# One static order for all five engines, the spatial bias on VectorE and the gate on GpSimd

## The chip, the cores and the metric

The kernel runs on one core of a Trainium2 chip. The metric is the device time of one execution in microseconds (us). Most executions of one kernel agree closely; a run over 1.5% above the fastest of its kernel is called slow, and ratios use fast runs alone. A profiled execution has a span (first to last instruction) of some 1.8 us less than its time (some 2.2 us in the two versions with the bias put back). The profiled run of the kernel before happened to be a slow one (182.71 us, span 180.9), some 5 us above its usual time.

## The reference, cut to what matters

Two parts follow each other. Attention with a decay goes over blocks of tokens with a running state; its output x feeds a gated MLP with a spatial mixing over the tokens of each of four batches.

```python
# attention, per batch and head, block by block
intra = (q @ k.T) * D @ v                  # D: lam**(i-j) where i >= j
inter = (q * lam**(i+1)) @ kv_state
kv_state = lam**block * kv_state + (k * lam**(block-1-i)).T @ v
# MLP, per batch
h = relu(x @ w_in); u, v = halves(h)
v_n = (v - mean(v)) / sqrt(var(v) + 1e-6)
v_s = w_spatial @ v_n + b_spatial
out = (u * v_s) @ w_out
```

The kernel does the attention in 12 steps of 256 tokens, three to a batch.

## The kernel before

Each step is loaded (k, q, v: 1.57 MB, of which k and v come in rows of 256 bytes), cast by GpSimd (kd is k times its decay, qc, vc), transposed by TensorE and copied by ScalarE (kT) and VectorE (qT). The program fixes the order of TensorE, GpSimd and SyncE by hand; the order of ScalarE and VectorE is left to the framework. The steps of the MLP are pv and pu (x times the two halves of w_in), vn (the normalised v), pvs (spatial mixing), po (output). An ask is the instruction by which an engine starts a transfer; the transfer lands later.

The parts that the change and the argument touch:

```python
def load_step(n):                         # SyncE asks: k in two halves, q, then v
    ...
    if n >= 2:
        load_v(n, nc.sync)
...
load_step(0)
load_v(0, nc.scalar, (0,))                # ScalarE asks for half of v 0 at once
load_step(1)
...
load_v(1, nc.sync, (1,))
for n in range(2, 4):
    load_step(n)
...
for g in range(NG):                       # decays of the queries
    last = nc.scalar.activation(out=lq[:, g, :], in_=qpos, func=AF.Exp, scale=logl[:, g:g + 1])
with tc.issue_after(last.ins):
    load_v(0, nc.scalar, (1,))            # the other halves, behind lq
    load_v(1, nc.scalar, (0,))
...
def pvs(b, f):
    ...
        for s in range(NBLK):
            nc.tensor.matmul(out=ps[:, i, 0:HW_], lhsT=vn..., rhs=wt_sb..., ...)
        nc.tensor.matmul(out=ps[:, i, 0:HW_], lhsT=oo128, rhs=bsp_bc[:, cols], ...)   # the bias
    nc.vector.tensor_tensor(out=gT..., in0=ps..., in1=uT..., op=ALU.mult)             # the gate
...
run("""
    mask ck:0 cq:0 ck:1 cv:0 win:1 cq:1 cv:1 c:2 win:0 wsp wout c:3 lk:4 lk:5 lk:6
    T:0 K:0 A:0 T:1 O:0 K:1 A:1 pv:0:0 O:1 T:2 K:2 ...
""")
```

## Time and profile before

| | before |
|---|---|
| time, median (range) | 177.0 us (176.21 to 178.74), 3 runs |
| TensorE busy (PE) | 145.4 us, 80% of the span of 180.9 |
| VectorE (DVE) | 106.0 us, 59% |
| ScalarE (ACT) | 77.3 us, 43% |
| GpSimd (POOL) | 53.2 us, 29% |
| transfers | 28.36 MB, done with all but stores at about 104 us |

The table is to be read with time in mind: none of these shares is near 100%, because the loads hold everything up in the first 44 us and TensorE is full later. The prediction shows the rows that say so.

### The profile page before, as it was taken

To read this page: it belongs to the slowest core of one execution; us is meant where nothing else is said; L and a number is where in the kernel's file an instruction comes from. 1 tells how busy PE (TensorE), PEld (TensorE's weight loads), DVE (VectorE), ACT (ScalarE), POOL (GpSimd) and SP (SyncE) were. 2 spreads that over 40 slices of the span, in tenths; PEclk is the share of its full clock that TensorE was granted. 3 is DMA by queue.
4 is the path that set the end of the run, shared out by engine and by line. 5 is a ranking of instruction groups with operands and counts; after the bars stand their busy time and mean duration, and the time that the engine had idled before them with its cause. 6 is when DMAs were issued, how large, how long until landed. Compare 5 with 4: busy or idle time off the path is not lost.

```text
span 180.9 us, 3629 instructions
## 1 busy us (share of the span) xinstructions
PE 145.4 (80%) x1528; PEld 95.2 (53%) x1540; DVE 106.0 (59%) x182; ACT 77.3 (43%) x88; POOL 53.2 (29%) x50
## 2 busy tenths in 40 slices
PE   0041699399869999997955999999999999999890
PEld 0031566176636665676742655567866645776430
DVE  0712988921652889579998447179994713834400
ACT  2940057237911045677450014756822257660051
POOL 2439639400555566207556702000000000000000
PEclk9999999969987999999997899999999999999997
DMA  3999999999999999999899900630000026000036
GB/s 79 266 224 239 212 243 224 194 202 200 239 226 218 253 216 270 321 263 196 220 238 224 236 5 0 235 116 4 0 4 0 0 104 248 0 0 5 0 126 222
DMA packets 68497, 28.36 MB, mean 157 GB/s; under 512 B 50560, under 2 KB 65536, under 8 KB 68480
## 3 DMA queue, kind: packets, MB, share of 16 engines
q1 hardware_dynamic: 62560, 24.25, 58.2%
q0 software_dynamic: 2512, 2.95, 9.4%
q10 hardware_dynamic: 3408, 0.92, 2.7%
q8 instruction: 12, 0.20, 0.5%
q14 instruction: 5, 0.04, 0.1%
HBM read 24.78 MB, written 6.29 MB: 172 GB/s over the span
## 4 chain that ended last, share of the span: by engine, by line
PE 53%; DVE 17%; DMA 12%; SPq 9%; ACT 3%; issue 1%; POOL 1%; ACTq 0%; POOLq 0%
PE pvs L344 17%; PE po L359 10%; DMA wsp_raw<-in_moe_w_spatial_dram 8%; PE pv L313 8%; PE pu L334 7%; SPq L78 5%; DVE a L228 5%; DMA v_in<-in_v_dram 5%; DVE vn L325 4%; PE pvs L346 3%; PE pt L199 3%; DVE gT L348 2%; SPq L80 2%; DVE st L319 2%; SPq L69 2%; DVE sd L254 2%
## 5 line engine op out<-in xcount | busy, mean ns | idle before, releaser
L344 PE MATMUL pvs<-wt_sb,vn 128*128 128x384 bf16 x192 | 39.8, 343 | 5.2 <-DVE vn L325 5.1
L228 DVE TENSOR_TENSOR a<-pam,amask 128x1024 bf16<-128x1024 f32 x24 | 28.5, 1211 | 3.4 <-PE pam L225 3.4
L183 POOL TENSOR_TENSOR kd<-k_in,ldec 128x1024 bf16<-128x1024 f32 x12 | 23.0, 1917 | 23.2 <-DMA k_in<-in_k_dram 16.2
L344 PEld LDWEIGHTS <-vn 128*128 128x128 bf16 x192 | 19.4, 103 | 19.6 <-DVE vn L325 6.3
L204 ACT ACTIVATE kT<-pt 128x1024 bf16<-128x1024 bf16 x12 | 12.2, 1021 | 38.9 <-PE pt L199 38.9
L348 DVE TENSOR_TENSOR gT<-pvs,uT 128x768 bf16<-128x768 f32 x16 | 15.3, 957 | 19.6 <-PE pvs L346 19.6
L334 PE MATMUL pu<-xT,win_sb 128*128 128x256 bf16 x192 | 24.0, 284 | 2.9 <-DMA win_sb<-in_moe_w_in_dram 2.9
L313 PE MATMUL pv<-win_sb,xT 128*128 128x512 bf16 x89 | 22.0, 380 | 1.9 <-ACT xT L288 1.6
L359 PE MATMUL po<-wout_sb,gT 128*128 128x512 bf16 x91 | 21.7, 379 | 1.4 <-DVE a L228 0.7
L319 DVE BATCH_NORM_STATS2 st<-vh 128x6 f32<-128x512 bf16 x24 | 15.4, 682 | 12.5 <-ACT vh L316 12.3
L334 PEld LDWEIGHTS <-win_sb 128*128 128x128 bf16 x192 | 19.2, 102 | 6.6 <-DMA win_sb<-in_moe_w_in_dram 3.0
L288 ACT ACTIVATE xT<-pat 128x1024 bf16<-128x1024 f32 x12 | 15.8, 1320 | 15.6 <-PE pat L285 15.4
L191 POOL CAST vc<-v_in 128x1024 bf16<-128x1024 f32 x12 | 12.8, 1066 | 28.1 <-DMA v_in<-in_v_dram 20.9
L372 ACT ACTIVATE o<-po 128x1024 f32<-128x1024 f32 x11 | 11.3, 1025 | 18.3 <-PE po L359 18.3
L336 ACT ACTIVATE uT<-pu 128x1024 bf16<-128x1024 f32 x12 | 12.2, 1021 | 10.1 <-PE pu L334 10.1
L316 ACT ACTIVATE vh<-pv 128x1024 bf16<-128x1024 f32 x12 | 12.2, 1021 | 8.2 <-PE pv L313 8.1
L199 PE MATMUL pt<-ident,kd 128*128 128x128 bf16 x96 | 8.2, 234 | 9.1 <-POOL kd L183 9.1
L359 PEld LDWEIGHTS <-gT 128*128 128x128 bf16 x96 | 9.1, 98 | 11.7 <-DVE gT L348 1.3
L313 PEld LDWEIGHTS <-xT 128*128 128x128 bf16 x96 | 8.9, 98 | 11.3 <-ACT xT L288 2.0
L188 POOL CAST qc<-q_in 128x1024 bf16<-128x1024 f32 x12 | 12.9, 1076 | 5.9 <-DMA q_in<-in_q_dram 5.7
L206 DVE TENSOR_TENSOR qT<-pt,lq 128x1024 bf16<-128x1024 bf16 x12 | 8.2, 684 | 10.7 <-ACT kT L204 10.7
L325 DVE TENSOR_SCALAR vn<-vh,mv,rstd 128x512 bf16<-128x512 bf16 x24 | 14.1, 629 | 0.3
(54 smaller groups left out, 142.0 us busy)
## 6 DMA issues: line engine op xcount, KB each, us to landing
k_in<-in_k_dram SPq DMA_DIRECT2D x24, 256.0 KB, 5.3
q_in<-in_q_dram SPq DMA_DIRECT2D x12, 512.0 KB, 6.7
out_dram<-o SPq DMA_DIRECT2D x11, 512.0 KB, 3.1
v_in<-in_v_dram SPq DMA_DIRECT2D x21, 256.0 KB, 6.5
wsp_raw<-in_moe_w_spatial_dram POOLq DMA_DIRECT2D x1, 1152.0 KB, 14.2
win_sb<-in_moe_w_in_dram POOLq DMA_DIRECT2D x2, 512.0 KB, 8.2
v_in<-in_v_dram ACTq DMA_DIRECT2D x3, 256.0 KB, 6.3
wout_sb<-in_moe_w_out_dram POOLq DMA_DIRECT2D x1, 512.0 KB, 17.4
```

What stands on the lines that cost most here:

```text
L183: nc.gpsimd.tensor_tensor(out=kd.rearrange("p c h d -> p h c d"), in0=s["k_in"], in1=ldec.unsqueeze(2).unsqueeze(3).broadcast_to((P, H, 2, ...
L188: nc.gpsimd.tensor_copy(out=qc.rearrange("p m h d -> p h m d"), in_=s["q_in"])
L199: nc.tensor.transpose(out=pt[:, j, g, c * P:(c + 1) * P], in_=src[:, c, 2 * g:2 * g + 2, :].rearrange("p h d -> p (h d)"), identity=ident)
L228: nc.vector.tensor_tensor(out=a_sb[:, i].rearrange("p h g c x -> p (h g) c x"), in0=pam.rearrange("p h g c x -> p (h g) c x"), in1=amask[: ...
L288: nc.scalar.activation(out=xT[b][:, r].rearrange("p g (c d m) -> p (g c) m d", c=2, m=2), in_=po.rearrange("p g c (m d) -> p (g c) m d", m ...
L313: nc.tensor.matmul(out=ps[:, j], lhsT=x[:, r, c, j * P:(j + 1) * P], rhs=win_sb[:, c, DH:DFF], start=(c == 0), stop=(c == NCH - 1))
L319: nc.vector.bn_stats(out=m["st6"][:, t, :], in_=vh[:, t, :])
L325: nc.vector.tensor_scalar(out=m["vn"][:, t, :], in0=vh[:, t, :], scalar1=mv[:, t, 0:1], scalar2=rstd[:, t:t + 1], op0=ALU.subtract, op1=AL ...
L334: nc.tensor.matmul(out=ps[:, f], lhsT=win_sb[:, c, f * P:(f + 1) * P], rhs=x[:, r, c, :], start=(c == 0), stop=(c == NCH - 1))
L344: nc.tensor.matmul(out=ps[:, i, 0:HW_], lhsT=m["vn"][:, s, f * P:(f + 1) * P], rhs=wt_sb[:, s, cols], start=(s == 0), stop=False)
L348: nc.vector.tensor_tensor(out=m["gT"][:, f, :].rearrange("p (i x) -> p i x", i=2), in0=ps[:, :, 0:HW_], in1=m["uT"][:, f, :].rearrange("p ...
L359: nc.tensor.matmul(out=ps[:, j], lhsT=gT[:, c, t * P:(t + 1) * P], rhs=wout_sb[:, c, :], start=(c == 0), stop=(c == NCH - 1))
```

## The change

The intent is to give each engine one static order, made by a list schedule, in which work of three batches interleaves; to take the bias matmuls from TensorE and the gate from VectorE; and to drop the rescaling of the state by using decays counted from the start of the batch. The diff, cut to its core:

```diff
-    ctx.enter_context(tc.manual_schedule(engines={PE, Pool, SP}))
+    ctx.enter_context(tc.manual_schedule(engines={PE, Pool, Activation, DVE, SP}))
 ...
+    def load_v(n):
+        load_kv("v", v, n, nc.scalar if n < 2 else nc.sync)
 ...
+    def key_decays(r): ...        # 6 exponentials instead of 1 (ldec), lm128 and l128 gone
+    def query_decays(r): ...      # 12 instead of 4 (lq)
 ...
-                nc.vector.tensor_tensor(out=sd, in0=prev, in1=lb, op=ALU.mult)
-                nc.vector.tensor_tensor(out=s_sb[:, c], in0=sd, in1=pkv[:, c], op=ALU.add)
+            nc.vector.tensor_tensor(out=s["s"][:, c], in0=prev, in1=s["pkv"][:, c], op=ALU.add)
 ...
-            nc.tensor.matmul(out=ps[:, i, 0:HW_], lhsT=oo128, rhs=bsp_bc[:, cols], ...)
+    def bias(b, f):
+            nc.vector.tensor_tensor(out=h[:, i], in0=ps["s", b, f]..., in1=bsp_bc..., op=ALU.add)
+    def gate(b, f):
+        eng = nc.vector if b == B - 1 else nc.gpsimd
+            eng.tensor_tensor(out=gT..., in0=h..., in1=uT..., op=ALU.mult)
 ...
+    order = """
+        k:0 q:0 k:1 q:1 k:2 q:2 v:2 k:3 q:3 v:3 bsp ld:0 v:0 lq:0 ld:1 ld:2 v:1 ck:0 k:4 lq:1
+        cq:0 q:4 T:0 lq:2 qT:0 ck:1 kT:0 A:0:0 cq:1 a:0:0 cv:0 wv v:4 k:5 q:5 wu ws K:0 T:1
+        ...
+    """
```

In the order, k, q, v and the w words are loads, ld and lq the decays, ck, cq, cv the casts. T (transposes), A (scores), K (key-value product), O (the part from the state) and V (the part within the block) are TensorE's steps of the attention; a and s are VectorE's mask and state, xT is ScalarE's copy of the result. In the MLP, vh, bn, rs and uT lead from pv and pu to vn and u, h is the bias, g the gate, o the output copy, out the store. Each engine takes its own words in this order and never goes past one that waits.

## The prediction

> **What bounds the kernel now.** I started at the page's busy shares in 40 slices, to see whether one engine bounds the whole span or several take turns.
>
> ```profile
> PE   0041699399869999997955999999999999999890
> DVE  0712988921652889579998447179994713834400
> PEclk9999999969987999999997899999999999999997
> DMA  3999999999999999999899900630000026000036
> ```
>
> A slice is 4.5 us. The transfers are full from the second slice to slice 23 (about 104 us) and idle afterwards; TensorE is full from slice 23 to the end and patchy before. So there are two stages: a start of some 44 us in which data arrive too slowly to fill TensorE, and then a long stage that is TensorE's own, with holes. The DMA page line says 68497 packets, 28.36 MB, so the loads are the same size after the change and still end not much before 100 us; I ask later whether that bites.
>
> Next, the table of stretches (start:end, length, then busy us of PE, PEld, DVE, ACT, POOL, granted clock, DMA share, GB/s), cut at the holes:
>
> ```profile
> 30.00:35.70 5.70, 2.67 (x32) 1.31 (x32) 5.17 (x11) 2.46 (x4) 3.49 (x3) 0.99 1.14 193
> 35.70:39.40 3.70, 3.63 (x24) 2.44 (x26) 1.55 (x4) 0.09 (x1) 0.00 (x0) 0.55 1.16 201
> 50.00:58.00 8.00, 6.80 (x41) 3.92 (x42) 3.27 (x4) 0.38 (x1) 4.27 (x4) 0.79 1.22 232
> 90.00:97.00 7.00, 3.40 (x66) 2.19 (x64) 6.60 (x10) 2.63 (x3) 4.74 (x4) 1.00 1.01 226
> 97.00:101.00 4.00, 3.52 (x13) 1.78 (x14) 2.44 (x6) 0.00 (x0) 1.67 (x3) 0.57 1.23 231
> 130.00:150.00 20.00, 19.56 (x212) 12.18 (x213) 11.48 (x16) 7.18 (x7) 0.00 (x0) 1.00 0.09 32
> ```
>
> The reader should see pairs: a hole (30 to 35.7, 90 to 97), and right behind it a stretch that looks full but ran at a clock of 0.55 to 0.57. A hole is paid for twice.
>
> Who is waited for, from the view of waits of TensorE:
>
> ```profile
> PE pt L199 <- POOL kd L183: 9.1, 1, 9.1
> PE pvs L344 <- DVE vn L325: 5.1, 4, 2.1
> PE pam L225 <- DVE qT L206: 4.6, 3, 3.2
> PE pkv L243 <- POOL vc L191: 4.5, 1, 4.5
> PE pu L334 <- DMA win_sb<-in_moe_w_in_dram: 2.9, 1, 2.9
> ```
>
> The first, fourth, fifth and most of the third lie before 44 us (start-up). After 44 us the waits are pvs 5.1, pam 1.5, pv 1.2, po 0.7 and 0.4: 8.9 us, nearly all for VectorE. Why VectorE is late is in the timeline around 94 us:
>
> ```profile
> 94.34 1.90 POOL L183 TENSOR_TENSOR kd<-k_in,ldec 128x1024 bf16<-128x1024 f32 x1 [1.14 <-DMA k_in<-in_k_dram]
> 94.58 2.84 DVE L325 TENSOR_SCALAR vn<-vh,mv,rstd 128x512 bf16<-128x512 bf16 x2
> 96.44 0.34 PE L344 MATMUL pvs<-wt_sb,vn 128*128 128x384 bf16 x1 [2.09 <-DVE vn L325]
> ```
>
> Two normalisations take 0.73 us when GpSimd is quiet (at 85.95), and here 2.84 us, beginning inside a GpSimd multiply. TensorE stands still behind them.
>
> **TensorE's own work**, from warm stretches: 16 transposes 0.89 us, 16 scores 0.55, 16 of K 0.37, inter 0.56, intra 0.57, a pv, pu or po step 1.73 to 1.75, a pvs half 0.97, a weight-transpose piece 0.84. Twelve steps: 10.7 + 6.6 + 3.7 + 5.6 + 6.8 + 20.8 + 21.0 + 20.8, plus 32 halves 31.0, plus 2.5 = 129.5 us. The bias matmul is the difference between a pvs period of 1.137 us (161.94 to 163.08) and 0.97: 0.167 x 32 = 5.3 us. Before: 134.8.
> At 44 us some 16.6 us of it was done, so 118 us remained, and the last po matmul ended at 176: 132 us. Lost: 14 us = 8.9 waits + clock (8 x 0.21 + 4 x 0.43 = 3.4) + some 1.5 in small gaps.
>
> **What the Trainium skill says.** "TensorE: Matmul & The Clock Gate", section "What's actually happening": the array's clock falls to half after an idle window of some 3.4 us and comes back after a busy one. The trace agrees (0.55 after a 2.9 us wait, six pvs matmuls in 1.92 instead of 0.97 us). "SBUF — State Buffer", section "SBUF: two separate sides": VectorE and GpSimd share a port pair under an exclusive lock, taken by VectorE instructions in a two-port mode or, against a GpSimd instruction that reads SBUF, with two SBUF inputs. The trace agrees: sd (two SBUF inputs) runs from 392 to 1945 ns and vn from 397 to 2083 ns, while the mask multiply and the state add, with one input in PSUM, stay at 1211 and 410. "GPSIMD Engine Reference", section "Performance versus the Vector engine", gives about 2.6 cycles an element for a two-input operation; here kd takes 1917 ns for 1024, 1.87 ns each, which I use. "DMA: Bandwidth & Descriptors", section "Queues, rings and completion order": each engine takes turns between queue rows, packet by packet. The trace fits: while weights ran from 28.8 us, issuing two k loads took 12.85 us.
>
> **The change, part by part.**
> - Bias matmuls out of TensorE: -5.3 us, nearly all after 44 us, on the path: the full 5.3.
> - Bias added by VectorE in place of the gate: 16 of the same form as gT (128x768, one input in PSUM), 957 ns: equal, 15.3 us out and in.
> - Gates of three batches on GpSimd: 12 x 768 x 1.87 ns = 1.44 us each, 17 us more on GpSimd (53 to 69 us). It is waiting for loads most of its time, so this is beside other work; but a chain pvs, bias, gate, po gets 1.4 us longer, and GpSimd holds the port pair longer. Last batch: 4 gates of some 0.85 us (768 elements at the rate of gT) on VectorE, +3.4.
> - Decays folded into absolute powers: the 16 sd multiplies (11.8 us, of which 16 x 0.425 = 6.8 is work and 5 is blocking) and amask (3.0) disappear. In: ten more small exponentials on ScalarE (8 of lq, 492 ns mean before), 4 to 5 us in the first 20 us. VectorE: 106.0 - 11.8 - 3.0 + 3.4 + 1 (one q cast) = 96. The fewer blocked instructions are worth part of the 8.9 us of waits.
> - Order: the weights win (second half) and wsp are asked for straight after the first at about 17 us instead of 27.6, and wout later. wsp landed at 42.6, which the chain of waits shows as 7.8% of the span; I expect about 32 to 38. In exchange k, q, v of step 3 come later, which suits the new order: pv, pu of batch 0 come first. TensorE's work in the new order before the third step's transposes adds to 19.4 us; I put that point at about 41 us, against 16.6 done at 44: 3 to 5 us gained, of which I count 2.
> - Holes after 44 us: the new order interleaves three batches (attention of batch 2 starts before pvs of batch 1), so a late vn need not stop TensorE, and its buffers are double. Of 14 us lost I expect 6 to 8 back, clock included.
> - Last stretch: final gates 1.2 us instead of 0.97 before po, last copies from separate banks: about even.
>
> Sum: 5.3 + 2 + 7 = 14, minus 1 to 2 for the longer gate chain and a fixed order that fits real arrival times imperfectly: 13. From 177.0 this gives 164. I subtract from the median, not from the profiled run (182.7 us, itself a slow one).
>
> **Rivals.**
> - The loads become the bound. Work left behind the last transposes (step 11) in the new order is 45.7 us, plus 0.9, a gate gap of 1 and a tail of 4.7 (po's end at 176 to 180.9): 52. Loads at 225 GB/s gave about 9.4 MB by 45 us; the rest, with the stores of batch 0 now ahead of steps 9 to 11 in the same queue, lands at about 103 to 108. Then the end is 157 to 162. For: every step's load lands only 0 to 4 us before its turn. Against: TensorE is unlikely to be that far by then. It sets the floor of my range at about 157.
> - The fixed order turns into waits: ScalarE and VectorE are pinned too, so one late load or one vn blocked by GpSimd (now 30% busier) holds up copies behind it, and the single buffers for vh, h and gT bite. Then only the bias is gained and a little: 170 to 172.
> - VectorE or GpSimd as bound: 96 and 69 us busy against 130 of TensorE; only locally, worth 2 to 3 us.
>
> **Range and chances.** Between the load floor and the pinned-order rival: 157 to 171, middle 164. For no gain over 2%, all of the holes would have to stay and some new ones come on top of the 5.3 us removed: 6%. Slower: 1%.
>
> **What would show it.** Right: TensorE busy without line L346's matmuls; no sd rows; vn wait of pvs under 2 us; only one or no stretch at half clock after 45 us; wsp landed before 39 us; last transposes (step 11) at 104 to 112 us. Wrong: TensorE waits for GpSimd's gates or for k, q, v casts after 60 us adding to over 6 us; a new half-clock stretch; transfers idle between 80 and 95 us because the stores stand in front of the loads.

## The result, and the profile after

The changed kernel takes 185.39 us (184.85 to 185.82, 4 runs), the kernel before 177.87 beside it. The ratio is 1.0432, 95% interval 1.0335 to 1.053: slower, where a gain of 7% was forecast. A ratio here is always the mean time of one kernel's fast runs over the mean of the other's of the same rounds, so it is not quite the ratio of the medians. (Where two experiments are compared with each other, I divide their ratios to the kernel before.)

The page's rows of busy tenths in 40 slices of 4.6 us each, of the changed kernel:

```profile
PE   0210000738999789999999999999999999999780
ACT  4201419313566782355564426465754254642051
PEclk9999999995799999999999999999999999999997
DMA  4999999999999997900005699995502000044045
```

TensorE does next to nothing in slices 4 to 7, up to 32 us, where the kernel before was already working. From slice 11 (46 us) on it is nearly full, at 7 to 9 tenths. (The row PEclk prints a 9 where the trace has no record of the clock; the first record here is at 38 us. The eight transposes at 8.16 us took 1.04 us, those at 60.39 us 0.61 us, so the nines of the first slices don't mean full speed.) The page's group rows confirm the second stage (columns: busy time, mean ns; then idle time of the engine just before):

```profile
L368 POOL TENSOR_TENSOR gT<-h,uT 128x768 bf16<-128x768 f32 x12 | 19.8, 1650 | 37.0 <-DVE h L361 31.3
L346 PE MATMUL pvs<-wt_sb,vn 128*128 128x384 bf16 x192 | 33.4, 326 | 0.0
```

No pvs matmul waits for vn any more (5.1 us before). So the time was lost at the start. The view of waits of TensorE names it (total, times, longest):

```profile
PE pam L216 <- ACT kT L194: 23.4, 1, 23.4
PE pt L186 <- POOL kd L164: 8.7, 2, 8.2
PE pkv L237 <- POOL vc L178: 3.1, 1, 3.1
```

One wait of 23.4 us, for one copy by ScalarE. The timeline shows what ScalarE did before that copy (start, duration; ACTq is its queue of asks for transfers):

```profile
5.26 0.49 ACT L129 ACTIVATE ldec<-loglam,krev 128x8 f32<-128x8 f32 x2
...
14.43 3.44 ACTq L71 DMA_DIRECT2D v_in<-in_v_dram  x2
...
17.92 1.70 ACT L133 ACTIVATE lq<-qpos,logl 128x256 bf16<-128x256 f32 x4 [12.17 <-DMA v_in<-in_v_dram]
...
22.30 4.60 ACTq L71 DMA_DIRECT2D v_in<-in_v_dram  x2
...
26.95 4.04 ACT L133 ACTIVATE lq<-qpos,lg_r,logl 128x256 bf16<-128x256 f32 x8 [6.56 <-DMA v_in<-in_v_dram]
...
32.39 1.00 ACT L194 ACTIVATE kT<-pt 128x1024 bf16<-128x1024 bf16 x1
```

ScalarE had its first decays ready at 5.75 us. Next in its order were two asks for v of step 0; they went out at 14.43 us and some 3 us later. Only then came lq, the other ldec, two more asks (22.3 to 26.9), eight more lq, and last kT, which had been ready to copy at about 10 us. The page's median time from ask to landing is 5.7 us for these four; each ask itself took about 0.4.

Why did an ask wait 8.7 us? The instruction listing of the compiled program tells what each one waits for. In this program the transfers that SyncE and ScalarE ask for share eight completion semaphores, handed out in turn, and an ask waits until the earlier transfer with the same semaphore has landed (cut to the four semaphores that matter):

```
SyncE    k_in_2 (second half)     waits DMAHW0
         v_in_2 (first half)      waits DMAHW2
         k_in_3 (second half)     waits DMAHW5
         v_in_3 (first half)      waits DMAHW7
ScalarE  v_in_0 (first half)      waits DMAHW0
         v_in_0 (second half)     waits DMAHW2
         v_in_1 (first half)      waits DMAHW5
         v_in_1 (second half)     waits DMAHW7
```

ScalarE's four asks stand behind transfers that SyncE itself asked for only at 8.71, 11.73, 16.04 and 19.56 us. By the trace's semaphore events these landed at 14.41, 17.47, 22.28 and 26.50 us, and ScalarE's asks went out at 14.43, 17.49, 22.30 and 26.52 us, each 0.02 us later. In the kernel before, ScalarE asked early and no exponential waited for an ask:

```profile
1.22 0.61 ACTq L69 DMA_DIRECT2D v_in<-in_v_dram  x1
...
6.37 0.38 ACTq L69 DMA_DIRECT2D v_in<-in_v_dram  x1
...
6.75 1.29 ACT L135 ACTIVATE lq<-qpos,logl 128x256 bf16<-128x256 f32 x3
```

The Trainium skill, "DMA: Bandwidth & Descriptors", section "Anatomy of one DMA — SWDGE (gpsimd) path", says that a semaphore wait of a transfer "happens on the issuing sequencer before dispatch". The section is about GpSimd's path; this trace shows the same for ScalarE's asks, and adds that the engine's computing behind the ask stands still with it: lq waited 12.17 us.

The stages, with the transposes of step 3 as the mark (the new order has 19.4 us of TensorE's work before them):

| | step 3's transposes start | from there to the end | span |
|---|---|---|---|
| predicted | about 41 | about 121 | about 162 |
| changed kernel | 60.4 | 123.5 | 183.9 |

(The predicted span is the 164 us of the prediction less the 1.8 us between time and span; the stage is the difference.) The long stage is nearly as forecast; the start is 19 us late.

### The profile page after: what moved, and what is told of

Same layout as the page of the kernel before. It is cut to its first block, busy times and chain, and to the rows that moved or that the text cites. A ratio compares the mean times of both kernels' runs of the same rounds, so it can differ in the third digit from the quotient of the medians.

```text
span 183.9 us, 3570 instructions
## 1 busy us (share of the span) xinstructions
PE 139.4 (76%) x1499; PEld 91.6 (50%) x1512; DVE 101.3 (55%) x172; ACT 82.9 (45%) x99; POOL 70.3 (38%) x60
## 4 chain that ended last, share of the span: by engine, by line
PE 57%; DMA 12%; DVE 11%; SPq 10%; ACT 3%; POOL 2%; issue 1%; ACTq 0%; POOLq 0%
PE pvs L346 14%; DMA v_in<-in_v_dram 11%; PE pv L300 10%; PE po L387 9%; PE pu L335 9%; SPq L71 6%; PE pt L186 5%; SPq L84 4%; PE pam L216 3%; DVE vn L327 3%; PE pat L275 3%; PE pat L264 3%; DVE h L361 2%; DMA out_dram<-o 1%; PE pkv L237 1%; DVE st L312 1%
## 5 line engine op out<-in xcount | busy, mean ns | idle before, releaser
L223 DVE TENSOR_TENSOR a<-pam,causal 128x1024 bf16<-128x1024 f32 x24 | 28.9, 1214 | 16.1 <-PE pam L216 16.1
L164 POOL TENSOR_TENSOR kd<-k_in,ldec 128x1024 bf16<-128x1024 f32 x12 | 23.2, 1931 | 31.7 <-DMA k_in<-in_k_dram 19.7
L368 POOL TENSOR_TENSOR gT<-h,uT 128x768 bf16<-128x768 f32 x12 | 19.8, 1650 | 37.0 <-DVE h L361 31.3
L346 PE MATMUL pvs<-wt_sb,vn 128*128 128x384 bf16 x192 | 33.4, 326 | 0.0
L216 PE MATMUL pam<-qT,kT 64*128 64x128 bf16 x192 | 10.4, 233 | 24.6 <-ACT kT L194 23.4
L346 PEld LDWEIGHTS <-vn 128*128 128x128 bf16 x192 | 18.1, 98 | 12.5
L361 DVE TENSOR_TENSOR h<-pvs,bsp_bc 128x768 f32<-128x768 f32 (+1 forms) x17 | 15.3, 907 | 14.7 <-PE pvs L346 14.6
L387 PE MATMUL po<-wout_sb,gT 128*128 128x512 bf16 (+1 forms) x95 | 22.1, 370 | 1.2 <-DVE gT L368 0.9
L335 PE MATMUL pu<-xT,win_sb 128*128 128x256 bf16 x192 | 22.5, 273 | 0.0
L216 PEld LDWEIGHTS <-kT 64*128 64x128 bf16 x192 | 6.0, 100 | 28.8 <-ACT kT L194 24.3
L312 DVE BATCH_NORM_STATS2 st<-vh 128x6 f32<-128x512 bf16 x24 | 16.2, 675 | 6.8 <-ACT vh L305 6.8
L395 ACT ACTIVATE o<-po 128x1024 f32<-128x1024 f32 x11 | 11.3, 1024 | 17.1 <-PE po L387 16.4
L327 DVE TENSOR_SCALAR vn<-vh,mv,rstd 128x512 bf16<-128x512 bf16 x24 | 16.2, 716 | 0.4
(51 smaller groups left out, 139.6 us busy)
## 6 DMA issues: line engine op xcount, KB each, us to landing
win_sb<-in_moe_w_in_dram POOLq DMA_DIRECT2D x2, 512.0 KB, 10.6
```

The costliest lines, as they stand in the source:

```text
L164: nc.gpsimd.tensor_tensor(out=s["kd"].rearrange("p c h d -> p h c d"), in0=s["k"], in1=ldec[:, 2 * r:2 * r + 2, :].rearrange("p c h -> p h ...
L216: nc.tensor.matmul(out=pam[:, hh, g2, c, :], lhsT=kblk(n, g, hh, c), rhs=qblk(n, g, hh, c), start=True, stop=True)
L223: nc.vector.tensor_tensor(out=s["a"][:, i].rearrange("p h g c x -> p (h g) c x"), in0=s["pam", i].rearrange("p h g c x -> p (h g) c x"), i ...
L312: nc.vector.bn_stats(out=st6[:, t, :], in_=vh[:, t, :])
L327: nc.vector.tensor_scalar(out=vn[:, t, :], in0=gm["vh", b][:, t, :], scalar1=mv[:, t, 0:1], scalar2=rstd[:, t:t + 1], op0=ALU.subtract, op ...
L335: nc.tensor.matmul(out=p[:, f], lhsT=win_sb[:, c, f * P:(f + 1) * P], rhs=xT[b][:, r, c, :], start=(c == 0), stop=(c == NCH - 1))
```

## The experiments

Theory A says that ScalarE, in its fixed order, stands at asks that wait for other transfers, and TensorE behind it. Rival B says that the data of the start arrive too late whoever asks. Rival C puts the loss into the moved work: gates on GpSimd, added work of VectorE. Unless it says otherwise, a diff is against the changed kernel. "Base" is the version of the experiment named. All results were correct against the reference. Where a run counts as slow, it stands in the median and range given here, but not in the ratio.

### Asking by SyncE in turn

```diff
-        load_kv("v", v, n, nc.scalar if n < 2 else nc.sync)
+        load_kv("v", v, n, nc.sync)
-        k:0 q:0 k:1 q:1 k:2 q:2 v:2 k:3 q:3 v:3 bsp ld:0 v:0 lq:0 ld:1 ld:2 v:1 ck:0 ...
+        k:0 q:0 k:1 v:0 q:1 v:1 k:2 q:2 v:2 k:3 q:3 v:3 bsp ld:0 lq:0 ld:1 ld:2 ck:0 ...
```

> The changed kernel with one edit: the v loads of steps 0 and 1 are asked for by SyncE, in turn between the k and q loads, instead of by ScalarE behind its first exponentials. Theory A (ScalarE stood in its own order at four v issues, each waiting for an earlier transfer, and with it the decays, kT of step 0 and TensorE, from 9 to 33 us): the v waits of ScalarE vanish, the first scores matmul starts at 16 to 19 us instead of 33.45, the transposes of step 3 at 40 to 47 us instead of 60.4, and the time falls by 13 to 20 us to 165 to 172. Rival B (the start is bound by the arrival of the data; who asks is of no weight): time within 3 us of 185.4. Rival C (the loss comes from gates on GpSimd and the added VectorE work in the long stage): within 3 us as well, or the start gets earlier and the end does not.

Measured: 174.70 us (174.57 to 175.19), ratio to before 0.9845 (0.9766 to 0.9923), so 5.6% below the changed kernel (0.9845 / 1.0432). The first scores matmul started at 14.49 us instead of 33.45, and ScalarE's waits for v are gone:

```profile
14.49 0.61 PE L216 MATMUL pam<-qT,kT 64*128 64x128 bf16 x8 [4.55 <-ACT kT L194]
...
48.44 0.61 PE L186 MATMUL pt<-ident,kd 128*128 128x128 bf16 x8
```

Rivals B and C fall as the main cause. But the gain is 10.7 us, not 13 to 20: the transposes of step 3 came at 48.4 us, later than the 40 to 47 expected. Something else holds the start.

### SyncE, but late

```diff
-        load_kv("v", v, n, nc.scalar if n < 2 else nc.sync)
+        load_kv("v", v, n, nc.sync)
```

> The changed kernel, the same v loads given to SyncE but left at their place, behind the loads of step 3 and the bias. ScalarE is free of issues, the v data of step 0 come later than in the changed kernel (about 28 to 32 us against 23.5). Theory A in its strong form (ScalarE's standing still alone): first scores at 16 to 19 us, and most of the gain of the in-turn version, 167 to 175. If late v data are the other half: first scores early but K of step 0 only at about 30 us, and 178 to 184. Rival B: about 185 or more.

Measured: 178.70 us (177.57 to 181.53, the last a slow run), ratio 1.0041 (0.9952 to 1.0131). ScalarE is free and the first scores start at 14.74 us, but then TensorE waits for the cast of v of step 0. Its timeline:

```profile
14.74 0.61 PE L216 MATMUL pam<-qT,kT 64*128 64x128 bf16 x8 [4.80 <-ACT kT L194]
30.76 0.64 PE L237 MATMUL pkv<-vc,kd 128*64 128x64 bf16 x16 [15.41 <-POOL vc L178]
```

So freeing ScalarE alone is worth some 7 us (6.7 of median, 3.7% by the ratios), although the v data came later than in the changed kernel (the cast of v of step 0 began at 29.67 us against 23.57); asking in time is worth 4 more. The second form of the expectation holds.

### ScalarE asks, but first

```diff
-        load_kv("v", v, n, nc.scalar if n < 2 else nc.sync)
+        load_kv("v", v, n, nc.scalar if n < 1 else nc.sync)
-        k:0 q:0 k:1 q:1 k:2 q:2 v:2 k:3 q:3 v:3 bsp ld:0 v:0 lq:0 ld:1 ld:2 v:1 ck:0 ...
+        v:0 k:0 q:0 k:1 q:1 v:1 k:2 q:2 v:2 k:3 q:3 v:3 bsp ld:0 lq:0 ld:1 ld:2 ck:0 ...
```

> The changed kernel with the v load of step 0 still asked for by ScalarE, but first of all loads, and that of step 1 by SyncE in turn behind the q load of step 1. If it is the place in the order that counts (an ask made while eight transfers are out waits for an earlier one, and ScalarE's later instructions with it): as the version with all asks on SyncE in turn, first scores matmul at 14 to 17 us, 173 to 176.5 us. If it is ScalarE asking at all: first scores later than 20 us, 178 or more.

Measured: 174.20 us (174.07 to 174.77), ratio 0.9804 (0.9754 to 0.9854), as with SyncE in turn; the first scores start at 15.43 us. Its timeline, ScalarE:

```profile
3.76 1.04 ACTq L71 DMA_DIRECT2D v_in<-in_v_dram  x2
4.89 1.28 ACT L129 ACT_TABLE_LOAD   x1 [0.93 <-DVE lg_r L121]
6.18 0.49 ACT L129 ACTIVATE ldec<-loglam,krev 128x8 f32<-128x8 f32 x2
6.58 1.69 ACT L133 ACTIVATE lq<-qpos,logl 128x256 bf16<-128x256 f32 x4
```

Two asks in 1.04 us and no standing still behind them. For v of step 0 it is the place in the order that counted, not the engine that asks; v of step 1 was moved to SyncE in this run.

### The kernel before with the late asks

Against the kernel before: v of steps 0 and 1 asked for by ScalarE after the loads of steps 0 to 3 in the program, lq behind the first pair of asks.

```diff
-    load_step(0)
-    load_v(0, nc.scalar, (0,))
-    load_step(1)
-    load_v(1, nc.sync, (1,))
-    for n in range(2, 4):
-        load_step(n)
+    for n in range(4):
+        load_step(n)
 ...                                       # behind ldec:
+        load_v(0, nc.scalar, (0, 1))
 ...                                       # lq behind it, and behind lq:
+        load_v(1, nc.scalar, (0, 1))
```

> The kernel before with only the asking order of the change: v of steps 0 and 1 asked for by ScalarE behind the first small exponentials and behind the program's k, q, v loads of steps 0 to 3, with the lq exponentials behind the first pair of issues. Theory A: K of step 0 moves from 16 us to 22 to 26 us, and the time rises by 5 to 10 us to 183 to 188. Rivals B and C: within 2 us of 177.9.

Measured: 196.52 us median; two of the four runs (198.06 and 199.01) count as slow, and the profiled one is the first of them. The fast runs give a ratio of 1.0972 (1.0859 to 1.1084). The asking order alone makes the kernel before slower than the changed kernel is. The direction is that of theory A, the size about twice the upper end of what I expected. The key-value product of step 0 moved from 16.07 to 24.39 us as forecast. Why the rest came on top was not tested; the trace (a slow run, as is that of the kernel before) fits with the lateness growing down GpSimd's order, which asks for the weights behind the casts of v: the spatial weights were asked for at 40.31 us (28.39 before) and transposed at 60.7 us instead of 42.6.

### The added exponentials later

Against SyncE in turn:

```diff
-        ... ck:0 k:4 lq:1 cq:0 q:4 T:0 lq:2 qT:0 ck:1 kT:0 A:0:0 ...
+        ... ck:0 k:4 cq:0 q:4 T:0 qT:0 ck:1 kT:0 lq:1 lq:2 A:0:0 ...
```

> The in-turn version, and the eight added lq exponentials with the table load moved behind kT of step 0 in ScalarE's order. If the added exponentials (some 6 us on ScalarE) are a second part of the lost start: first scores at 10 to 12 us and 2 to 5 us less than the in-turn version. If the start is then bound by the v data and the weights: first scores early, time within 1.5 us of the in-turn version.

Measured: 174.73 us (173.45 to 174.99), ratio 0.9825 against 0.9845: no gain. The first scores start at 11.92 us instead of 14.49, and TensorE then waits 3.65 us for v. So the added exponentials cost nothing there: the v data are the later of the two. I keep this version as the base of the next four. Its timeline shows the next obstacle:

```profile
30.19 0.40 PE L216 MATMUL pam<-qT,kT 64*128 64x128 bf16 x8
35.97 0.43 PE L237 MATMUL pkv<-vc,kd 128*64 128x64 bf16 x8 [5.38 <-POOL vc L178]
36.32 3.21 PE L300 MATMUL pv<-win_sb,xT 128*128 128x512 bf16 x8
```

TensorE stands 5.38 us at the key-value product of step 2, and the pv step after it takes 3.21 us instead of 1.90: the trace records half the clock from 35.6 to 39.0 us. GpSimd, whose cast is waited for, waited 11.29 us for the v data of step 2, asked for by SyncE at 16.12 us: some 17 us to land. All 2.2 MB of early weights were asked for between 16.07 and 18.57 us.

### Spatial weights asked for later

Against that base:

```diff
-        ... cv:0 wv v:4 k:5 q:5 wu ws K:0 ... V:1 cv:2 v:6 ...
+        ... cv:0 wv v:4 k:5 q:5 wu K:0 ... V:1 cv:2 ws v:6 ...
```

> The same base, with one edit: the spatial weights are asked for by GpSimd behind the cast of v of step 2 instead of 10 us before it. Theory: the second loss at the start is that weights asked for all at once at 16 to 18 us starve the v load of step 2 (17 us to land), and TensorE's fixed order stands behind it from 30.6 to 36 us and runs at half clock afterwards. Then that wait shrinks below 2 us, the transposes of step 3 come at 40 to 44 us instead of 47.6, and the time falls by 3 to 7 us, 168 to 172. Rival: bandwidth is the limit, the wait only moves to step 3's loads or to the spatial weights: within 1.5 us of 174.7.

Measured: 168.60 us (167.10 to 168.83), ratio 0.9472 (0.938 to 0.9565): 3.6% below its base. The same place in its timeline:

```profile
30.60 0.32 PE L237 MATMUL pkv<-vc,kd 128*64 128x64 bf16 x8 [1.12 <-POOL vc L178]
30.84 1.90 PE L300 MATMUL pv<-win_sb,xT 128*128 128x512 bf16 x8
...
40.79 0.61 PE L186 MATMUL pt<-ident,kd 128*128 128x128 bf16 x8
```

The wait is 1.12 us, the second half of v of step 2 lands 11.7 us after its ask instead of 17.4 (semaphore events of the two traces), pv runs at full clock, and step 3's transposes start at 40.79 us, where the prediction had put them. The spatial weights, asked for 13 us later (30.49 against 17.74), cost a wait of 0.8 us. This is the second cause: what the order asked for too early starved what TensorE needed first.

### TensorE's order around the late load

Against the same base: the key-value product and the output of step 2 behind the second pv and the first two pu steps.

```diff
-        ... vh:0:0 K:2 a:2:1 pv:0:1 s:2:0 bn:0:0 O:2 ck:3 k:7 vh:0:1 V:2 pu:0:0 xT:2 ...
+        ... vh:0:0 a:2:1 pv:0:1 bn:0:0 ck:3 k:7 vh:0:1 pu:0:0 ... pu:0:1 uT:0:1 K:2 s:2:0 O:2 V:2 xT:2 ...
```

> The same base, weights asked for as there, but TensorE's order lets the second pv and two pu steps of batch 0 go ahead of the key-value products of step 2, which need the late v load. Theory (a fixed order that puts a late operand at the head): TensorE has work for the wait of 5.4 us, transposes of step 3 at 41 to 45 us, time 169 to 172.5. Rival: the first pu then waits for its own weights: within 1.5 us of 174.7.

Measured: 172.11 us (171.68 to 172.32), ratio 0.9688: 1.4% below the base, step 3's transposes at 45.66 us. So the same hole can also be mended from TensorE's side, with less than half the effect.

### Bias back on TensorE

Against the base with the exponentials later: matmuls with oo128 and a bf16 bias as before, VectorE gates from PSUM, no gate on GpSimd.

```diff
+            nc.tensor.matmul(out=p[:, i, 0:HW_], lhsT=oo128, rhs=bsp_bc[:, ...], start=False, stop=True)
-            nc.vector.tensor_tensor(out=h..., in0=ps["s", b, f]..., in1=bsp_bc..., op=ALU.add)
+            nc.vector.tensor_tensor(out=gT..., in0=ps["s", b, f]..., in1=uT..., op=ALU.mult)
```

> The version with the start mended and the exponentials later (174.73 us), and in it the bias put back on TensorE as 32 matmuls, with VectorE gating straight from PSUM; no gates on GpSimd. If the bias matmuls lie on the path in the long stage, as predicted: 4 to 6 us more, 178.5 to 180.8. If taking them away was paid back by the longer chain bias, gate, po, or by GpSimd's gates blocking VectorE: within 2 us of 174.7.

Measured: 179.66 us (178.54 to 181.70, the last a slow run), ratio 1.0083, 2.6% above the base. As expected in size, but not a clean test: step 3's transposes moved from 47.6 to 50.3 us, probably because the bias transfer now went with the early weights. It was repeated on the better base below.

### All gates on VectorE

```diff
-        eng = nc.vector if b == B - 1 else nc.gpsimd
+        eng = nc.vector
```

> The same base (174.73 us), with the gates of all four batches on VectorE, none on GpSimd. VectorE gets 12 x 0.96 = 11.5 us more work, GpSimd 19.8 us less. If the gates on GpSimd are free, as predicted: 0 to 3 us slower. If their hold on the port pair is what lengthens VectorE's normalisations and so the path: faster by over 1.5 us.

Measured: 175.63 us (175.17 to 177.41), ratio 0.9908 against the base's 0.9825: 0.8% slower, within what "free" allows. The groups of the normalisation on VectorE, base first, then this version (the second number is the mean in ns):

```profile
L327 DVE TENSOR_SCALAR vn<-vh,mv,rstd 128x512 bf16<-128x512 bf16 x24 | 16.7, 734 | 0.4
```

```profile
L327 DVE TENSOR_SCALAR vn<-vh,mv,rstd 128x512 bf16<-128x512 bf16 x24 | 12.1, 544 | 0.4
```

With GpSimd's gates vn is longer, 734 ns against 544, but in sum (VectorE has fewer gates in return) it costs nothing on the path. Rival C falls here too.

### The best version again, and the bias on top of it

The version with the spatial weights asked for later was run again with five rounds, as the base of three runs on the same chip.

> The best version so far again (168.6 us), as the base of the three runs beside it on the same chip: 167 to 170 us, 4 to 6.5% faster than the kernel before.

Measured: 167.46 us (166.47 to 168.64), ratio 0.9449 (0.9402 to 0.9496).

The edit of the bias experiment, on this base (the bias transfer goes with the late weights):

> That base, with the bias back on TensorE and VectorE gating from PSUM. The earlier undoing cost 4.9 us, but 2.7 us of it arose before the transposes of step 3, because the bias transfer then went along with the early weights. Here it goes with the late ones. If the bias matmuls are worth their 5.3 us on the path: 173 to 175. If part is paid back by the longer chain bias, gate, po (the last gates before po alone cost 0.9): 171 to 172.5. If they are hidden: under 170.

Measured: 170.56 us (169.86 to 173.01, the last a slow run), ratio 0.9611, so 1.7% or 2.9 us above the base: a little below the range in which part is paid back. Some 0.4 of the 2.9 lie outside the span (time less span is 2.1 to 2.2 us in the runs of this version, 1.7 to 1.9 in those of the base), and the trace does not show why. TensorE was busy 143.9 us here and 139.6 in the base, so 4.3 us of work go. The ends of the two timelines show what is paid back; base first:

```profile
154.42 4.72 PE L387 MATMUL po<-wout_sb,gT 128*128 128x512 bf16 x25 [0.93 <-DVE gT L368]
```

```profile
157.10 5.53 PE L384 MATMUL po<-wout_sb,gT 128*128 128x512 bf16 x28
```

With the bias on TensorE the last po steps run through. Without it they start 4.4 us earlier (152.68 against 157.10) but stand 0.93 us for the last gate, and from their start to the end of the span it is 12.0 us instead of 10.6.

### Loads ahead of the stores

On the best version:

```diff
-        ... s:7:1 T:8 o:0:2 out:0:2 k:9 q:9 v:9 k:10 q:10 v:10 k:11 q:11 v:11 A:7:0 ...
+        ... cv:6 k:9 q:9 v:9 k:10 q:10 v:10 rs:1:0 ... cq:7 k:11 q:11 v:11 ... o:0:0 out:0:0 ...
```

> That base, with the loads of steps 9 to 11 asked for ahead of the stores of batch 0 instead of behind them. The prediction named idle transfers at 80 to 95 us as a sign of error, and the changed kernel has them. If they cost time: over 1.5 us faster. If TensorE has work from other batches meanwhile, as its busy row says: within 1 us of the base.

Measured: 185.26 us (183.81 to 185.76), ratio 1.0432: 10% slower than its base, which neither case expected. Its timeline says why:

```profile
96.87 6.87 SPq L406 DMA_DIRECT2D out_dram<-o  x3
```

```profile
102.31 1.02 ACT L395 ACTIVATE o<-po 128x1024 f32<-128x1024 f32 x1 [19.24 <-DMA out_dram<-o]
```

There are two output buffers. The third output copy of ScalarE needs the first store to have landed; SyncE now had that store behind the asks for loads, which followed each other almost without a gap until 96.76 us; ScalarE stood 19.24 us at that copy, and TensorE 14.51 us behind ScalarE, then at half the clock. So idle transfers between 80 and 95 us, which the prediction took as a sign of error, cost TensorE nothing then (in the changed kernel it was busy 14.95 of these 15 us), and filling them in this way did. It is theory A once more, made by accident in another place.

### Both mendings of the late load

> That base with TensorE's other order of batch 0 as well (pv and pu ahead of the key-value products of step 2). If the late v load is still in TensorE's way: 1 to 2.5 us faster. If asking for the spatial weights later has already removed that wait (1.1 us is left of it): within 1 us of the base, or slower, as the xT of step 2 now comes later.

The edits are those of the two experiments above, taken together. Measured: 172.02 us (170.06 to 173.14; three of the six runs count as slow), ratio 0.9617: 1.8% slower than the best version, fast runs alone. Step 3's transposes start at 42.5 instead of 40.3 us, and TensorE then waits 2.4 us for qT of step 3. In TensorE's new order the xT of step 2 comes later, as feared. That this makes VectorE late with qT is likely but was not tested further.

## Why the prediction was wrong

**The step that failed** is the one headed "Order": "I put that point at about 41 us, against 16.6 done at 44: 3 to 5 us gained". The point, step 3's transposes, came at 60.4 us. The working counted TensorE's work and the landing of the weights, and did not ask when ScalarE's kT and the v data of the first steps would be there. It did not read ScalarE's new order as a queue: I listed ten more exponentials on ScalarE (the diff has eleven), 4 to 5 us, and passed over the four asks for v that stand among them. TensorE then waited 23.4 us for one kT. The runs put these amounts in place of the gain:

- ScalarE standing at asks that wait for SyncE's transfers, and v of steps 0 and 1 asked for late: 10.7 us (185.39 to 174.7), some 7 of it from ScalarE's standing still alone. Moving the exponentials that I did count gained nothing.
- The weights asked for together at 16 to 18 us: 6.1 us (174.73 to 168.6). I had named this as a gain ("In exchange k, q, v of step 3 come later, which suits the new order") and did not see that v of step 2 would be among the starved, at the head of TensorE's order. In the base with only the asks mended, the spatial weights did land at 34.1 us (17.7 + 16.4), as forecast, and it did harm.

With both mended the kernel takes 167.5 to 168.6 us, inside the range that was given for the changed kernel and 3.5 to 4.6 us above its middle. Of that, 2.4 us are the bias term (2.9 instead of 5.3); the rest is not assigned.

**The pinned-order rival** described this mechanism ("one late load ... holds up copies behind it"), but I gave it 170 to 172 us, which still is a gain; the kernel became 7.5 us slower. I looked for it in the long stage, at vn and at single buffers, and not in the start, where transfers are full.

**Bias off TensorE.** "On the path: the full 5.3". The sign was right. TensorE's busy time fell by 4.3 us and the time by 2.9, because the last po steps then wait 0.93 us for the longer chain and the tail after their start is 1.4 us longer in all. The term was mis-sized by nearly half.

**Gates on GpSimd.** Free on the path, as said. One takes 1650 ns, not 1440: I took the rate from kd. That kd is cheaper because its second input is a broadcast is a guess; no run tests it.

**VectorE.** Busy 101.3 us instead of 96: sd and amask went as forecast, but vn got longer, 16.2 us instead of 14.1, and the statistics a little (16.2 against 15.4).

**Holes after 44 us.** pvs no longer waits for vn; TensorE's waits after 60 us add to 3.2 us against 8.9 before; the only recorded stretch at reduced clock before the end of the work is that at the start, 0.66 between 40 and 50 us. Measured as in the prediction, time to the end over TensorE's listed work, the loss was 136.9 - 118.2 = 18.7 us before (to the end of the span) and 123.5 - 110.1 = 13.4 after: 5.3 us back, where 6 to 8 were given. (The listed work is some 4 to 5 us too small in both: TensorE was busy 114.4 us of those 123.5.) The 5.3 is uncertain by as much again, since the profile before is of the slow run. The prediction has the same flaw: it read its loss of 14 us off a run of 182.7 us and took the 7 us that it hoped to regain from the median of 177.0. Up to 5.7 us of that loss was not in the median run, so the term may have been too large from the start; no fast profile of the kernel before can settle it.

**The loads as the bound** did not come about: transfers were idle from 80 to 95 us and TensorE was not.

**The signs.** In the changed kernel the spatial weights landed at 44.8 us, not before 39, and the transposes of step 11 came at 129.6 us, not at 104 to 112; both follow from the late start.

**The clock.** The prediction says that the trace agrees with an idle window of some 3.4 us. The trace's stretches at half clock do last 3.41 us, but the three before 100 us each follow a stretch of that length in which TensorE still worked: 0.67 us (from 32.23), 1.51 us (from 49.30) and 1.01 us (from 93.67). So holes of 2 to 3 us were enough, shorter than the window. The prediction's sums take the clock as the trace has it, so this changes none of them.

## What to carry to other kernels

In a static order, an ask for a transfer is an instruction that can wait, and everything behind it in that engine's order waits with it; so look for each ask among computing instructions at what it may wait for, and put it first, or on an engine that computes nothing. Ask for transfers in the order in which the engine that bounds the kernel needs them, at the start above all: here 1.2 MB of weights, asked for 13 us too early, made a load of 256 KB that was needed at once land after 17.4 us instead of 11.7. And when a schedule is judged, first check where the first matmul of each kind starts: the first part of the loss was one wait of 23.4 us, visible in one line.

## What the Trainium skill lacked or had wrong

- The main page, "Trainium Kernel Development and Optimization", section "Key Constraints", says that asking from several engines "only saves the sequencer's issue time". It lacks the cost: asks on a computing engine made ScalarE's exponentials wait 18.7 us in two waits here, and moving them to SyncE, in turn, was worth 10.7 us.
- "DMA: Bandwidth & Descriptors", section "Queues, rings and completion order", has the turns between queues but no figure for what a small load suffers beside large ones on another queue: 256 KB of v took up to 17.4 us to land beside 2.2 MB of weights, against a median of 5.6 us in the same run.
- "GPSIMD Engine Reference", section "Performance versus the Vector engine", was right where I set it aside: its 2.6 cycles an element, at the 1.2 GHz that the main page gives GpSimd (section "NeuronCore Architecture"), would be an estimate of 1.66 us for a gate of 768 elements, and 1650 ns was measured; kd, with a broadcast input, took 1931 ns for 1024, which is less an element than the page says.
- "TensorE: Matmul & The Clock Gate", section "What's actually happening", lacks how idle a window has to be: here the clock fell to half after stretches of 3.41 us in which TensorE was busy for 0.67, 1.01 and 1.51 us.
